# Short low-half products of two feed-forward units on the two row halves of the TensorE array

## The chip, the cores and the metric

The kernel runs on one core of a Trainium2 chip. The metric is the device time of the whole kernel in microseconds (us), taken as the median of several executions. One more execution is recorded by the hardware profiler; all views of the profile come from it.

## What is computed

The reference takes x (2048 tokens of 448 channels) and returns the sum of x, a spectral filter on its layer norm (a two-dimensional real FFT, a product with complex weights, and the inverse FFT), and a mixer with a feed-forward part:

```python
h = gelu(layernorm(x) @ w1)              # w1: 448 x 448
hs = shifted(h) @ w2                     # four channel groups, shifted by +1, -1, +2, -2 tokens
x1 = x + hs
h2 = gelu(layernorm(x1) @ w3) @ w4       # w3: 448 x 1792, w4: 1792 x 448
return x + spectral(layernorm(x)) + x1 + h2
```

## The kernel before

Single-precision products are made of half-precision ones: each operand is split into a high and a low half, and three of the four products are added in PSUM (high by high, weight high by data low, weight low by data high).

The work around the change is the feed-forward part. Its 2048 tokens form 8 groups `G` of 256, its 1792 hidden channels 7 pieces `fp` of 256; a *unit* is one pair (G, fp), so there are 56. For each unit, `front` makes the w3 products into one PSUM bank (128 hidden channels by 256 tokens, for two halves `ff`), and evacuates it: ACT applies the Gelu (L726) and takes the high half (L728), DVE takes the low half (L729). `back` then multiplies with w4 into the accumulators `acc` (L808). In groups 5, 6 and 7 some units (`SEVEN`) go through `sums` instead: the Gelu (L738) writes to SBUF, DVE forms sums (L740, L741), ACT and DVE split them (L744, L745), and `seven` (L778) makes seven smaller products in the place of eight. At the end of their group DVE adds these side sums to x (L786) and the accumulators too (L815).

The 448 rows of w3 are three blocks of 128 and one of 64. For the last 64 rows the tiles hold two copies: `w3p[:, 3]` (high halves) and `w3p[:, 7]` (low halves) hold rows 384 to 447 of w3 on partitions 0 to 63 and again on 64 to 127, and block 3 of `x2all` holds the data's high halves on partitions 0 to 63 and its low halves on 64 to 127. So two products are enough for this block, each over all 128 partitions, and a unit has 2 x (3 x 3 + 2) = 22 products, all recorded at the helper's line L400:

```python
for t in ts:
    for wi, xi in ((0, 0), (0, 4), (4, 0)) if t < 3 else ((0, 0), (4, 0)):
        T.matmul(ps_out, wp[:, wi + t, cols], xT[:, xi + t, tok],
                 start=t == 0 and wi + xi == 0, stop=t == 3 and wi == 4)
```

`mlp` runs the units of some groups. `ahead` says how many fronts are written before the back of a unit, `tags` which PSUM banks the fronts take in turn ("mm" has two banks, "mm" and "tr" together four). It is called five times: for group 0, for groups 1 and 2 (beside the forward transform, `step1`, L567), for groups 3 and 4 (beside the chunks, L622, L639 and L667, and their ACT and DVE work at L629, L630, L644, L655, L670), for group 5 (beside the inverse, L688 and L709), and for groups 6 and 7. Everything in `mlp` but the evacuations has the low priority `FILL`, so a scheduler that plays through a timeline ahead of the run puts these products wherever the work of higher priority leaves TensorE free; evacuations have the highest, `EVAC`. The order on each engine is then fixed. `behind(...)` asks that an instruction come after a given other one.

`ln2` prepares the data of the feed-forward part: it centres on POOL or ACT (L501, L499), splits, and writes `x2all` through a transposing DMA. `powers` (L260) and `w_scale_end` (L587, L591) contain a few tiny products that find scales.

Of the kernel before, what the change touches and what calls it, by code (L numbers as in the profile page):

```python
# [13 lines left out]
F16 = mybir.dt.float16  # L14
# [11 lines left out]
TURN = [3, 1, 0, 2]  # L26
DONE = {c: [c - 2] for c in range(2, 12)} | {12: [10, 13], 13: [11, 12, 14, 15]}
FIRST = 2
WARM = 26
ZPRE = 2.0 ** -7  # L30
UPRE = 2.0 ** -3
# [2 lines left out]
AH = 2  # L34
# [5 lines left out]
EVAC, FILL = 0, 100000  # L40
# [85 lines left out]
def body(tc, nc, x, wf, w1, w2, w3, w4, c_g, c_n, c_small, out):  # L126
    V, A, P, T, SY = nc.vector, nc.scalar, nc.gpsimd, nc.tensor, nc.sync
    PSUM = bass.MemoryType.PSUM

    @contextlib.contextmanager  # L130
    def prio(base):
        kept = tc.cur_priority
        tc.cur_priority = max(base, at.get(base, 0))
        yield
        at[base] = tc.cur_priority
        tc.cur_priority = kept
# [24 lines left out]
    pw = pool("pw")  # L161
# [6 lines left out]
    def xb(b):  # L168
        return xt[b // 2][:, b % 2]
# [4 lines left out]
    def at_token(b):  # L174
        return (b + FIRST) % NB

# [40 lines left out]
    def load_w3(ts):  # L217
        for t in ts:
            if t < 3:
                SY.dma_start(w3raw[:, t], w3[128 * t:128 * t + 128])  # L220
            else:
# [5 lines left out]
    load_w3([2])  # L227
    x2mem = pw.tile([128, 10 * F], F16, name="x2mem")
    x2all = [x2mem[:, 2 * F * j:2 * F * j + 2 * F].rearrange("p (t n) -> p t n", t=7) for j in (1, 0, 2, 3)]
    w4half = [x2mem.bitcast(F32)[:, 2 * F:2 * F + 4 * D].rearrange("p (f n) -> p f n", f=4),  # L230
              p1.tile([128, 10, D], F32, name="w4half")]
    w4v = w4.rearrange("(f p) n -> p f n", p=128)
# [139 lines left out]
    after = {}  # L372

    @contextlib.contextmanager
    def behind(*key):
        key = key if len(key) > 1 else key[0]
        with contextlib.ExitStack() as st:
            for i in after[key]:
                st.enter_context(tc.issue_after(i))
            yield  # L380
# [16 lines left out]
    def mlp_in(ps_out, wp, cols, xT, tok, ts=range(4)):  # L397
# [6 lines that stand above are left out]
    w3p = pa.tile([128, 8, F], F16, name="w3p")  # L404
# [77 lines left out]
    def ln2(bs, engines, late=None):  # L482

        n, b0 = len(bs), bs[0]
        mv = stats([xb(b) for b in bs], f"b{b0}")
        a = pc.tile([128, 4], F32, tag="vb", bufs=2, name=f"vb{b0}")[:, :n]
        r = pc.tile([128, 4], F32, tag="vs", bufs=2, name=f"vs{b0}")[:, :n]
        o, y = [], []
        nm = pc.tile([128, 4], F32, tag="nm", bufs=2, name=f"nm{b0}")[:, :n]
        P.tensor_scalar(out=nm, in0=mv[:, :n, 0], scalar1=-1.0, scalar2=None, op0=ALU.mult)  # L490
        for m in range(0, n, 2):
            w = stage(f"y{b0 + m}", 8 * 448, (b0 + m) // 2 % 2, F16)
            o.append(w[:, 0:4 * D].bitcast(F32).rearrange("p (i n) -> p i n", i=2))
            y.append(w[:, 4 * D:8 * D].rearrange("p (i n) -> p i n", i=2))
            for i in range(2):
                e = engines[m + i]
                c = nm[:, m + i:m + i + 1]
                if e is A:
                    A.activation(out=o[-1][:, i], in_=xb(b0 + m + i), func=AF.Identity, bias=c)  # L499
                else:  # L500
                    e.tensor_scalar(out=o[-1][:, i], in0=xb(b0 + m + i), scalar1=1.0, scalar2=c,  # L501
                                    op0=ALU.mult, op1=ALU.add)
        V.tensor_scalar(out=a, in0=mv[:, :n, 1], scalar1=eps12, scalar2=None, op0=ALU.add)
        rsqrt(r, a, n, f"b{b0}")
        for i in range(n):
            b, h, x_ = b0 + i, y[i // 2][:, i % 2], o[i // 2][:, i % 2]
            k = r[:, i:i + 1]
            with behind(*late) if late else contextlib.nullcontext():
                u = A.activation(out=h[:, 0:D], in_=x_, func=AF.Copy, scale=k)
            V.scalar_tensor_tensor(out=h[:, 448:512], in0=x_[:, 384:448], scalar=k, in1=h[:, 384:448],  # L510
                                   op0=ALU.mult, op1=ALU.subtract)
            v = V.scalar_tensor_tensor(out=h[:, 512:896], in0=x_[:, 0:384], scalar=k, in1=h[:, 0:384],
                                       op0=ALU.mult, op1=ALU.subtract)
            d = SY.dma_start_transpose(out=x2all[b // 4][:, :, 128 * (b % 4):128 * (b % 4) + 128], in_=h)
            after[f"b{b0}"] = u.ins, v.ins, d.ins

    def unscale(p, part):
        t = part.rearrange("p (b n) -> p b n", b=2)
# [194 lines left out]

    acc, hs = {}, {}

    def front(G, fp, tag):
        tok = slice(256 * (G % 2), 256 * (G % 2) + 256)
        pm = bank(tag, f"pw3_{G}{fp}")
        for ff in range(2):
            f = 2 * fp + ff  # L720
            mlp_in(pm[:, 256 * ff:256 * ff + 256], w3p, slice(128 * f, 128 * f + 128), x2all[G // 2], tok)
        with prio(EVAC):
            if fp in SEVEN.get(G, ()):
                hs[G, fp] = sums(G, fp, pm)
                return
            A.activation(out=pm, in_=pm, func=AF.Gelu_apprx_tanh, scale=r3)  # L726
            h = pw.tile([128, 2, 512], F16, tag="hf", bufs=3, name=f"hf{G}{fp}")
            i = A.activation(out=h[:, 0], in_=pm, func=AF.Copy, scale=h3)  # L728
            j = V.scalar_tensor_tensor(out=h[:, 1], in0=pm, scalar=h3, in1=h[:, 0], op0=ALU.mult, op1=ALU.subtract)  # L729
            after["f", G, fp] = i.ins, j.ins  # L730
        hs[G, fp] = h
# [56 lines left out]
    def back(G, fp):  # L788
        first, end = fp == ORD[G][0], fp == ORD[G][-1]
        if first:  # L790
            acc[G] = [bank("acc", f"acc{G}{i}") for i in range(2)]
            if G == 7:
                acc[G].append(bank("tr", "acc72"))
        h = None
        if fp in SEVEN.get(G, ()):
            seven(G, fp, end)
        else:
            h = hs.pop((G, fp))
        for i in range(2):
            b = 2 * G + i  # L800
            c = D // 2 if b == NB - 1 else D
            parts = [(slice(o, o + c), acc[G][i + o // c][:, 0:c]) for o in range(0, D, c)]
            for r, to in parts if h is not None else ():
                with behind("m", G, fp) if G == 7 and end and ("m", G, fp) in after else contextlib.nullcontext():
                    for f in (2 * fp, 2 * fp + 1):
                        for n, (hi, wi) in enumerate(PASS):
                            o = 256 * (f % 2) + 128 * i
                            m = T.matmul(to, h[:, hi, o:o + 128], w4p[0][:, wi, f, r],  # L808
                                         start=first and f % 2 == 0 and n == 0, stop=end and f % 2 == 1 and n == 2,
                                         skip_group_check=G in SEVEN)  # L810
                after["m", G, fp] = (m.ins,)
            if end:
                with prio(EVAC):
                    for r, to in parts:
                        V.scalar_tensor_tensor(out=xb(b)[:, r], in0=to, scalar=p34[:, min(G, 1):min(G, 1) + 1],  # L815
                                               in1=xb(b)[:, r], op0=ALU.mult, op1=ALU.add)
                        if G > 4:
                            SY.dma_start(ov[:, at_token(b), r], xb(b)[:, r])

    def mlp(Gs, hook=None, ahead=1, tags=("mm",)):  # L820
        with prio(FILL):
            todo = [(G, fp) for G in Gs for fp in ORD[G]]
            done = 0
            for n, (G, fp) in enumerate(todo):
                while done < min(n + 1 + (ahead if todo[n] != (7, 5) else 1), len(todo)):
                    front(*todo[done], tags[done % len(tags)])
                    if hook:
                        with prio(EVAC):
                            hook(*todo[done])
                    done += 1  # L830
                back(G, fp)


# [55 lines left out]
    n = 2  # L889
# [30 lines left out]
    with behind("g", 1), behind("na", 2):  # L920
        for k in range(4):
            r = slice(0, 128 if k < 3 else 64)
# [64 lines left out]
            with behind("f", G, fp):  # L987
                w4_split(2 * fp + 4)

    mlp([0], hook=w4_rest, ahead=AH, tags=("mm", "tr"))  # L990
    ln2(range(4, 8), [P, A, P, A])
    for b in range(8, 12):
        w2_tile(b)
# [23 lines left out]
            with behind("f", G, fp):  # L1017
                go()

    mlp([1, 2], hook=between, ahead=AH, tags=("mm", "tr"))  # L1020
    wl = stage("wl", 8 * DF, 1)
    for b in range(0, NB, 2):
        do_fold(b)
# [35 lines left out]
    for n in range(17):  # L1059
# [4 lines left out]
        if n:  # L1064
            b = bs[n - 1]
# [12 lines left out]
                    go()  # L1078

    mlp([5], hook=w4_late)  # L1080
    mlp(range(6, 8), hook=w4_late, ahead=2)
    for name in ("pv", "pz", "pa", "pw", "px", "pc", "ps"):
        close(name)

# [23 lines left out]
```

## Time and profile before

| | us |
|---|---|
| median of three runs | 408.19 |
| lowest and highest | 408.05, 408.2 |
| profiled execution, whole | 408.05 |
| profiled execution, first to last instruction (span) | 406.3 |

The clock that TensorE was granted is 0.998 of full speed on average. In the profile, PE is TensorE's products, PEld its weight loads, DVE VectorE, ACT ScalarE, POOL GpSimd and SP SyncE. A row of the timeline has start, length, engine, line, operation, destination and sources, shape and count; a merged row counts from the first start to the last end. A product's length is its latency: the next one starts before it ends, so rates are read from starts.

### The profile page before, as it was taken

The page shows a single profiled execution, that of the slowest core. Times are in us where ns is not written, and L with a number is a line of the kernel's source. Part 1 is how long each engine was busy: PE and PEld are TensorE (multiplying, and loading weights), DVE is VectorE, ACT ScalarE, POOL GpSimd, SP SyncE. Part 2 cuts the span into 40 slices and gives each one's busy share as a digit, 9 for nine tenths or more (in the row PEclk, how much of TensorE's full clock was granted, in tenths as well). Part 3 has the DMA queues.
Part 4 walks back from the last instruction along what each step waited for, and adds up shares of the span by engine and source line. Part 5 has one row for each costly group of instructions (what it writes and reads, how often), then busy time and mean ns, then how long its engine had stood idle before and what let it go on. Part 6 is the DMA issues. An engine that isn't in the chain of part 4 may idle for free.

```text
span 406.3 us, 8732 instructions
## 1 busy us (share of the span) xinstructions
PE 399.9 (98%) x3391; PEld 297.2 (73%) x3391; DVE 333.6 (82%) x702; ACT 255.1 (63%) x433; POOL 100.4 (25%) x158
## 2 busy tenths in 40 slices
PE   8999999999999999999999999999999999999996
PEld 3555555865667877777878878777677779998995
DVE  5898799898947887988698888965999999965645
ACT  4788889874568857655698878853354544353431
POOL 6859910111146946500021111110000000000000
PEclk9999999999999999999999999999999999999999
DMA  8978975567489661637256556510011023100101
GB/s 280 389 272 160 249 152 138 122 121 163 95 225 266 234 191 46 219 95 185 72 144 164 162 142 161 139 27 2 24 69 70 24 90 92 47 2 2 45 2 45
DMA packets 54596, 52.07 MB, mean 128 GB/s; under 512 B 35678, under 2 KB 48542, under 8 KB 54556
## 3 DMA queue, kind: packets, MB, share of 16 engines
q1 hardware_dynamic: 54556, 51.53, 46.0%
q8 instruction: 26, 0.43, 0.4%
q14 instruction: 14, 0.11, 0.1%
HBM read 38.28 MB, written 3.67 MB: 103 GB/s over the span
## 4 chain that ended last, share of the span: by engine, by line
PE 87%; POOL 5%; DMA 2%; DVE 2%; ACT 2%; issue 1%; SPq 0%; POOLq 0%; ACTq 0%
PE pw L400 33%; PE acc L808 23%; PE pw L478 6%; PE side L778 4%; PE acc L778 3%; PE pu L667 3%; PE ps L567 3%; PE pe L688 2%; PE pp L622 2%; PE px L639 2%; PE py L709 2%; PE pw L420 2%; DMA w1s<-w 1%; POOL xt L336 1%; DMA h<-x2mem 1%
## 5 line engine op out<-in xcount | busy, mean ns | idle before, releaser
L400 PE MATMUL pw<-x2mem,w3p 128*128 128x256 f16 x1232 | 151.3, 273 | 0.0
L400 PEld LDWEIGHTS <-w3p 128*128 128x128 f16 x1232 | 118.9, 98 | 19.3
L808 PE MATMUL acc<-w4p,hf 128*128 128x448 f16 (+1 forms) x516 | 104.4, 348 | 0.0
L808 PEld LDWEIGHTS <-hf 128*128 128x128 f16 x516 | 50.1, 98 | 37.6
L726 ACT ACTIVATE pw<-pw,pe 128x512 f32<-128x512 f32 x42 | 27.4, 654 | 26.8 <-PE pw L400 26.6
L729 DVE SCALAR_TENSOR_TENSOR hf<-pw,h,hf 128x512 f16<-128x512 f32 x42 | 31.3, 746 | 12.9 <-ACT hf L728 12.7
L478 PE MATMUL pw<-w2p,h 128*128 128x448 f16 x176 | 35.8, 353 | 0.9 <-DMA h<-x2mem 0.9
L420 PE MATMUL pw<-w1p,xT 128*128 128x448 f16 x176 | 34.9, 352 | 0.1
L648 POOL TENSOR_TENSOR z<-te 128x450 f32<-128x450 f32 x16 | 15.7, 983 | 70.8 <-DVE te L646 65.9
L728 ACT ACTIVATE hf<-pw,h 128x512 f16<-128x512 f32 x42 | 28.9, 687 | 5.0 <-PE acc L808 4.0
L478 PEld LDWEIGHTS <-h 128*128 128x128 f16 x176 | 17.0, 98 | 17.0 <-DMA h<-x2mem 2.0
L744 ACT ACTIVATE hz<-g,h 128x896 f16<-128x896 f32 x14 | 14.6, 1044 | 23.1 <-DVE g L741 23.1
L420 PEld LDWEIGHTS <-xT 128*128 128x128 f16 x176 | 17.1, 99 | 16.1 <-DVE xT L394 0.4
L778 PEld LDWEIGHTS <-hz 128*128 128x128 f16 x294 | 28.3, 98 | 0.6
L629 ACT ACTIVATE pf<-pp 64x450 f16<-64x450 f32 x32 | 17.4, 544 | 12.5 <-DVE pf L630 9.7
L630 DVE TENSOR_TENSOR pf<-pp,pf 64x450 f16<-64x450 f32 x32 | 19.9, 622 | 5.1 <-ACT pf L629 4.7
L745 DVE SCALAR_TENSOR_TENSOR hz<-g,h,hz 128x896 f16<-128x896 f32 x14 | 16.1, 1148 | 6.8 <-ACT hz L744 6.8
L550 POOL TENSOR_TENSOR f<-xr 128x452 f32<-128x452 f32 x16 | 19.7, 1251 | 0.6
L558 DVE TENSOR_TENSOR xh<-f,xh 128x452 f16<-128x452 f32 x16 | 14.3, 916 | 5.7 <-ACT xh L557 5.7
L644 ACT ACTIVATE te<-px 64x450 f32<-64x450 f32 x32 | 17.3, 541 | 1.2 <-PE px L639 0.6
L738 ACT ACTIVATE g<-pw,pe 128x512 f32<-128x512 f32 x14 | 9.6, 683 | 11.3 <-PE pw L400 11.3
L547 POOL TENSOR_TENSOR xr<-xf 128x452 f32<-128x452 f32 x8 | 9.2, 1156 | 22.3 <-issue 16.4
(188 smaller groups left out, 705.7 us busy)
## 6 DMA issues: line engine op xcount, KB each, us to landing
wc<-wf SPq DMA_DIRECT2D x32, 225.0 KB, 3.7
wl<-wf SPq DMA_DIRECT2D x8, 450.0 KB, 4.3
xt<-x SPq DMA_DIRECT2D x8, 448.0 KB, 7.1
xf<-x SPq DMA_DIRECT2D x8, 448.0 KB, 4.6
loads<-x SPq DMA_DIRECT2D x7, 448.0 KB, 4.0
out<-xt SPq DMA_DIRECT2D x13, 224.0 KB, 1.9
w3raw<-w SPq DMA_DIRECT2D x3, 896.0 KB, 10.8
gn<-c_g SPq DMA_DIRECT2D x16, 128.0 KB, 3.0
```

Source lines behind the costliest of these rows:

```text
L400: T.matmul(ps_out, wp[:, wi + t, cols], xT[:, xi + t, tok], start=t == 0 and wi + xi == 0, stop=t == 3 and wi == 4)
L420: m = T.matmul(pm[:, :D], xTs[g][:, xi + t, 128 * i:128 * i + 128], w1p[:, wi + t], start=t == 0 and p == 0, stop=t == 3 and p == 2)
L478: T.matmul(pm[:, :D], h[:, k], w2p[:, w], start=n == 0, stop=n == 10)
L550: P.tensor_tensor(out=f[:, :, k:k + 2].rearrange("p b s d -> p s b d"), in0=u[:, :, 0], in1=u[:, :, 1], op=op)
L629: A.activation(out=hi, in_=src, func=AF.Copy)
L630: V.tensor_tensor(out=lo, in0=src, in1=hi, op=ALU.subtract)
L644: A.activation(out=e[64 * h:64 * h + 64], in_=px_[64 - 64 * h:128 - 64 * h, :2 * DF], func=AF.Copy)
L726: A.activation(out=pm, in_=pm, func=AF.Gelu_apprx_tanh, scale=r3)
L728: i = A.activation(out=h[:, 0], in_=pm, func=AF.Copy, scale=h3)
L729: j = V.scalar_tensor_tensor(out=h[:, 1], in0=pm, scalar=h3, in1=h[:, 0], op0=ALU.mult, op1=ALU.subtract)
L778: m = T.matmul(to, h[:, hi, 128 * blk:128 * blk + 128], b[wi], start=new and n == 0, stop=n == 2 and (last if blk in (2, 5, 3, 0) else end ...
L808: m = T.matmul(to, h[:, hi, o:o + 128], w4p[0][:, wi, f, r], start=first and f % 2 == 0 and n == 0, stop=end and f % 2 == 1 and n == 2, sk ...
```

## The change

The low half of w3's last 64 rows is no longer multiplied with both halves of the data, but with the high half alone, over 64 partitions. The four such products of two neighbouring units (two halves `ff` each) are written one after another: the first unit's on partitions 0 to 63, the second's on 64 to 127, into different banks. For the second unit the data's high half is needed on partitions 64 to 127, so POOL copies it into a new tile `x2d`, once for each four blocks of tokens. A unit that has no partner (`alone`) keeps its 22 products. The two units of a pair are evacuated together, after the short products. `ahead` is 2 in all calls, where it was 1 for groups 3 to 5 and at one unit of group 7.

```diff
@@ body
+    x2d = pw.tile([128, 4, 512], F16, name="x2d")
@@ ln2
+        if b % 4 == 3:
+            P.tensor_copy(out=x2d[64:128, b // 4], in_=x2all[b // 4][0:64, 3])
@@ front
-    def front(G, fp, tag):
+    def front(G, fp, tag, alone):
         tok = slice(256 * (G % 2), 256 * (G % 2) + 256)
         pm = bank(tag, f"pw3_{G}{fp}")
         for ff in range(2):
             f = 2 * fp + ff
-            mlp_in(pm[:, 256 * ff:256 * ff + 256], w3p, slice(128 * f, 128 * f + 128), x2all[G // 2], tok)
+            for t in range(4):
+                for wi, xi in ((0, 0), (0, 4), (4, 0)) if t < 3 else ((0, 0), (4, 0)) if alone else ((0, 0),):
+                    m = T.matmul(pm[:, 256 * ff:256 * ff + 256], w3p[:, wi + t, 128 * f:128 * f + 128],
+                             x2all[G // 2][:, xi + t, tok], start=ff == 0 and t == 0 and wi + xi == 0,
+                                 stop=ff == 1 and t == 3 and wi == 4, skip_group_check=True)
+        after["w3"] = (m.ins,)
+        return pm
+
+    def last(units):
+        for ff in range(2):
+            for n, (G, fp, pm) in enumerate(units):
+                r = slice(64 * n, 64 * n + 64)
+                tok = slice(256 * (G % 2), 256 * (G % 2) + 256)
+                x_ = x2d[r, G // 2, tok] if n else x2all[G // 2][r, 3, tok]
+                f = 2 * fp + ff
+                with behind("w3"):
+                    m = T.matmul(pm[:, 256 * ff:256 * ff + 256], w3p[r, 7, 128 * f:128 * f + 128], x_, start=False,
+                                 stop=ff == 1, skip_group_check=True)
+
+    def evac(G, fp, pm):
         with prio(EVAC):
             ...
@@ mlp
-    def mlp(Gs, hook=None, ahead=1, tags=("mm",)):
+    def mlp(Gs, hook=None, ahead=2, tags=("mm",), single=1):
         with prio(FILL):
             todo = [(G, fp) for G in Gs for fp in ORD[G]]
-            done = 0
+            done, open_ = 0, []
             for n, (G, fp) in enumerate(todo):
-                while done < min(n + 1 + (ahead if todo[n] != (7, 5) else 1), len(todo)):
-                    front(*todo[done], tags[done % len(tags)])
-                    if hook:
-                        with prio(EVAC):
-                            hook(*todo[done])
+                while done < min(n + 1 + ahead, len(todo)):
+                    alone = not open_ and (done == len(todo) - 1 or done < single)
+                    open_.append((*todo[done], front(*todo[done], tags[done % len(tags)], alone)))
                     done += 1
+                    if alone or len(open_) == 2:
+                        if not alone:
+                            last(open_)
+                        for u in open_:
+                            evac(*u)
+                            if hook:
+                                with prio(EVAC):
+                                    hook(*u[:2])
+                        open_ = []
                 back(G, fp)
```

More of the change, by code (lines that the diff above doesn't have):

```diff
@@ L28 @@
 FIRST = 2
+HF = 3
 WARM = 26
@@ L726, in front @@
             A.activation(out=pm, in_=pm, func=AF.Gelu_apprx_tanh, scale=r3)
-            h = pw.tile([128, 2, 512], F16, tag="hf", bufs=3, name=f"hf{G}{fp}")
+            h = pw.tile([128, 2, 512], F16, tag="hf", bufs=HF, name=f"hf{G}{fp}")
             i = A.activation(out=h[:, 0], in_=pm, func=AF.Copy, scale=h3)
@@ L988, in w4_rest @@
                 w4_split(2 * fp + 4)
-    mlp([0], hook=w4_rest, ahead=AH, tags=("mm", "tr"))
+    mlp([0], hook=w4_rest, tags=("mm", "tr"))
     ln2(range(4, 8), [P, A, P, A])
@@ L1018, in between @@
                 go()
-    mlp([1, 2], hook=between, ahead=AH, tags=("mm", "tr"))
+    mlp([1, 2], hook=between, single=1, tags=("mm", "tr"))
     wl = stage("wl", 8 * DF, 1)
@@ L1080, in body @@
     mlp([5], hook=w4_late)
-    mlp(range(6, 8), hook=w4_late, ahead=2)
+    mlp(range(6, 8), hook=w4_late, single=1)
     for name in ("pv", "pz", "pa", "pw", "px", "pc", "ps"):
```

## The prediction

> **What bounds the kernel now.** I read the page first, then the table by stretches, the chain of waits, and single stretches of the timeline. The page says that one engine is full and which group fills it.
>
> ```profile
> span 406.3 us, 8732 instructions
> PE 399.9 (98%) x3391; PEld 297.2 (73%) x3391; DVE 333.6 (82%) x702; ACT 255.1 (63%) x433; POOL 100.4 (25%) x158
> PE 87%; POOL 5%; DMA 2%; DVE 2%; ACT 2%; issue 1%; SPq 0%; POOLq 0%; ACTq 0%
> ...
> L400 PE MATMUL pw<-x2mem,w3p 128*128 128x256 f16 x1232 | 151.3, 273 | 0.0
> L400 PEld LDWEIGHTS <-w3p 128*128 128x128 f16 x1232 | 118.9, 98 | 19.3
> ```
>
> TensorE (PE) is busy 98% of the span and carries 87% of the chain that ended last; L400, the w3 products that are changed, is its largest group and is never idle before an instruction (0.0). A busy PE could still run below its rate, so I look at starts. Three consecutive groups of the timeline, columns start and length:
>
> ```profile
> 132.98 2.56 PE L400 MATMUL pw<-x2mem,w3p 128*128 128x256 f16 x22
> 135.38 2.43 PE L808 MATMUL acc<-w4p,hf 128*128 128x448 f16 x12
> 137.65 1.50 PE L567 MATMUL ps<-csm,xh 128*128 128x128 f16 x24
> 138.99 2.56 PE L400 MATMUL pw<-x2mem,w3p 128*128 128x256 f16 x22
> ```
>
> From start to start, 22 w3 products of one unit take 2.40 us, 109.1 ns each; 12 w4 products 2.27 us, 189 ns each; 24 products of 128 columns, each with a weight load of its own, 1.34 us, 55.8 ns each. The groups follow each other without a gap. So a removed w3 product is worth 109 ns of the end time, not 273, which is its latency. The stretches say where something else is nearly full too (columns: sum PE, PEld, DVE, ACT, POOL, then clock, DMA share, GB/s):
>
> ```profile
> 195.00:283.00 88.00, 88.00 (x893) 70.63 (x891) 72.51 (x119) 67.23 (x120) 15.73 (x16) 1.00 0.44 117
> 283.00:345.00 62.00, 62.00 (x590) 48.49 (x588) 58.42 (x135) 28.66 (x52) 0.00 (x0) 1.00 0.18 61
> ```
>
> PE is busy for the whole of both, at clock 1.00. That cuts both ways: every slot saved counts, and every new wait counts too, since PE has no idle time to pay it from. DVE is at 94% from 283 to 345 us, and DVE and ACT at 82% and 76% from 195 to 283.
>
> **Products saved.** With one unit alone at the front of each of the five calls, and one at the end of the three calls with 14 units, 8 of the 56 units stay as they are and 48 form 24 pairs. A pair loses four full products (one for each half of two units) and gains four short ones. If the two row halves work at once, these take two slots: 4 x 109 - 2 x 109 = 218 ns less, 24 x 0.218 = **-5.2 us**. The four weight loads fit: at 55.8 ns each they need 223 ns.
>
> **Entering and leaving the half-array form.** No row shows 64-row products. The nearest are the two one-row products of L591; the same two-product step on all rows, L260, stands for comparison:
>
> ```profile
> 78.27 1.15 PE L400 MATMUL pw<-x2mem,w3p 128*128 128x256 f16 x9
> 79.26 0.28 PE L260 MATMUL pm<-pt,ones 128*128 128x1 f32 x2
> 79.40 0.92 PE L478 MATMUL pw<-w2p,h 128*128 128x448 f16 x4
> ...
> 189.61 1.11 PE L808 MATMUL acc<-w4p,hf 128*128 128x448 f16 x5
> 190.65 0.38 PE L591 MATMUL wpb<-wt,ones 1*128 1x1 f32 x2
> 190.96 0.74 PE L808 MATMUL acc<-w4p,hf 128*128 128x448 f16 x3
> ...
> 79.15 0.30 PEld L260 LDWEIGHTS pm<-pt,ones 128*128 128x128 f32 x2
> 79.29 0.77 PEld L478 LDWEIGHTS <-h 128*128 128x128 f16 x5
> 190.65 0.29 PEld L591 LDWEIGHTS wpb<-wt,ones 1*128 1x128 f32 x2 [0.37 <-issue]
> 190.95 0.49 PEld L808 LDWEIGHTS <-hf 128*128 128x128 f16 x4
> ```
>
> L260 starts where nine w3 slots end (78.27 + 9 x 0.109 = 79.25) and hands over 0.14 us later, at 79.40. L591 follows five w4 slots ending at 189.61 + 5 x 0.189 = 190.555, starts 0.095 us late, and hands over at 190.96: 0.405 us from end to start, 0.265 more. The load rows agree: the load after L260 starts while L260's loads run (79.29, inside 79.15 to 79.45), that after L591 only when they are over (190.95 after 190.94). So 0.265 us is the upper end of a trip into the short form and back; the lower is 0. I take 0.17 us, 0.095 in and a little less out; the rest I put down to the uncovered single-precision load, 0.30 us for two in L260's row, where L400 loads in 98 ns. 24 x 0.17 = **+4.1 us**, bounds 0 and 6.4. Below nothing is excluded: the trip adds no work that the full products had.
>
> The Trainium skill, TensorEngine Tiling (Array Packing), section Key Properties, says that changing the tiling mode drains the engine; the trace agrees, with those 0.095 us before L591. By the rule with that price for each change, the term would be 24 x 2 x 0.095 = 4.6 us in place of 4.1.
>
> **Groups torn apart.** The four short products are separate instructions of low priority; where the scheduler puts another product between them, a trip is paid again and an overlap lost. It does so to today's units:
>
> ```profile
> 226.13 0.27 PE L400 MATMUL pw<-x2mem,w3p 128*128 128x256 f16 x1
> 226.24 0.74 PE L639 MATMUL px<-pf,gn 128*128 128x225 f16 x6
> 226.82 0.38 PE L400 MATMUL pw<-x2mem,w3p 128*128 128x256 f16 x2
> 227.03 2.43 PE L808 MATMUL acc<-w4p,hf 128*128 128x448 f16 x12
> ```
>
> Here six chunk products stand before a unit's last two. I take two such breaks over the 12 or so pairs between 195 and 345 us, at 0.17 to 0.28 us: **+0.5 us**, bounds 0 and 2.
>
> **Later evacuation.** Today a unit is evacuated when its own products end, and before its bank is wanted again come one `back` and another `front`: 2.27 + 2.40 = 4.7 us. Paired, the first unit waits for the second and the short products, and then only one `back` (2.27 us) stands before the `front` that wants its bank, where units have just the two "mm" banks: groups 3, 4 and 5. Of the unit that ended at 227.03:
>
> ```profile
> 228.11 1.10 ACT L644 ACTIVATE te<-px 64x450 f32<-64x450 f32 x2
> 229.30 1.04 PE L400 MATMUL pw<-x2mem,w3p 128*128 128x256 f16 x8
> 229.68 0.64 ACT L726 ACTIVATE pw<-pw,pe 128x512 f32<-128x512 f32 x1
> 230.33 0.83 PE L667 MATMUL pu<-gn,zb 128*128 128x128 f16 x12
> 230.35 0.69 ACT L728 ACTIVATE hf<-pw,h 128x512 f16<-128x512 f32 x1
> 231.07 0.75 DVE L729 SCALAR_TENSOR_TENSOR hf<-pw,h,hf 128x512 f16<-128x512 f32 x1
> ```
>
> Its Gelu starts at 229.68, after other ACT work such as L644, and its bank is free when L729 ends, 231.82: 4.8 us after the products. The three steps themselves are 0.64 + 0.69 + 0.75 = 2.1 us, so even without a queue the chain just fits the 2.27 us. The next `front` starts at 229.30 today; it would wait 2.5 us here, unless chunk products such as L667 fill in. Those take about a third of PE between 195 and 283 us (28 us of 88: 286 w3 products at 0.109 and 152 w4 products at 0.189 leave that), so some 1.1 us stands beside each `back`. Between a need of 2.1 and 4.8 us and a cover of 3.4, I take 0.4 us a pair for the six pairs of groups 3 and 4, 2.4 us, and 0.6 us for the two such pairs of group 5, where DVE is at 94%. The counts just used:
>
> ```profile
> 195.00:283.00 88.00, 36.52 (x286) 27.21 (x287) 1.00 0.44 117
> 195.00:283.00 88.00, 31.53 (x152) 14.73 (x152) 1.00 0.44 117
> ```
>
> In groups 6 and 7 most units use the seven-product form. Their bank is free after the Gelu, but their halves come later:
>
> ```profile
> 380.62 2.57 PE L400 MATMUL pw<-x2mem,w3p 128*128 128x256 f16 x22
> 382.92 2.03 PEld L778 LDWEIGHTS <-hz 128*128 128x128 f16 x21
> 385.04 2.56 PE L400 MATMUL pw<-x2mem,w3p 128*128 128x256 f16 x22
> 386.13 1.15 DVE L745 SCALAR_TENSOR_TENSOR hz<-g,h,hz 128x896 f16<-128x896 f32 x1 [1.17 <-ACT hz L744]
> ```
>
> The unit's products end at 383.02 and L745 at 387.28, 4.26 us later. Today two backs and two fronts cover that; paired, one back (383.02 to 385.04, 2.02 us) and one front of 20 products (2.18 us), and the low half is wanted only by the third product: about even. I take 0.1 us a pair for six pairs, 0.6 us. In groups 0 to 2 units rotate over four banks: nothing. Together **+3.6 us**, bounds 0 and 9.
>
> **At nothing.** Four POOL copies of the high halves, each waiting for the transposes to land: POOL is busy 25%, and a unit alone and two fronts stand ahead of the first reader. Queued behind a copy on POOL are the next centring of `ln2` and the folds; if the folds came late, up to 1 us. ACT and DVE get as many instructions as before. The last unit is evacuated alone as today.
>
> **Sum.** -5.2 + 4.1 + 0.5 + 3.6 = +3.0 us on the profiled execution's 408.05, so 411.0; the median, 408.19, lies 0.14 above that execution, so **411.2 us**. By the bounds: from -5.2 to 1.2 + 2 + 9 + 1 = +13.2.
>
> **The rivals.** *The overlap is paid in full.* Trip free, breaks costing 0.2, waits 1.2 because chunk products fill them: -3.8, so 404.4. It decides once trip plus the rest is under 218 ns a pair; with my 4.1 us of breaks and waits, 0.17 us a pair, the trip must be under 0.05 us. For it: one-row single-precision products are a far stand-in for 64-row half-precision ones. Against: two independent rows point to a trip of over 0.1 us.
>
> *Loads of a half wait for that half's product.* The second product of each half then starts a load late, 98 ns for both halves together: 24 x 0.098 = +2.4, so 413.6. Full-array loads don't wait so (98 ns inside 109 in L400's two rows). This is the rule of the Trainium skill, TensorE: Matmul & The Clock Gate, section The mechanism: loads overlap running products only if the row group differs; no run here shows it for two groups.
>
> *The halves don't work at once.* Then the 5.2 us never come: +8.2, so 416.4. Nothing in this trace shows two products sharing the array.
>
> *It cancels.* A trip near 0.05 us with my waits leaves no change.
>
> **How the numbers follow.** About 0.2% (0.8 us) is what a measurement of this kernel tells from no change. Forecast 0.43, with a range of its own of 409.2 to 414; overlap in full, with its part ways, 0.27; loads that wait 0.12; no overlap 0.12; cancelling 0.06. Slower is 0.43 + 0.12 + 0.12 = 0.67. The range leaves the outermost tenth of each side: 403.9 to 417.0.
>
> **What would show it.** The short products get their own line: in each group of four, the second should start within about 60 ns of the first, and the step from the last full product's slot to the next full product should last 0.39 us. PE should show idle time before `front` in the stretch from 195 to 345 us, released by DVE's last step of an evacuation (today's L729). It would be wrong if the groups last under 0.3 us and PE stays gapless (faster), or if the second short product starts a full 109 ns after the first.

## The result, and the profile after

The changed kernel takes 413.60 us (four runs, 412.83 to 414.29) against 408.12 us before; the ratio is 1.0135, with a 95% interval of 1.0115 to 1.0155. The forecast was 411.2 us, in a range of 403.9 to 417.0. The profiled execution of the changed kernel took 413.91 us, with a span of 412.1 us, 5.8 us more than the span before; line numbers have moved (the full w3 products are L729 now, the short ones L743, the w4 products L833, the last evacuation step L754, the POOL copy L519).

The page of the changed kernel: span, busy time, the chain that ended last by engine, and the group of the full w3 products with its loads.

```profile
span 412.1 us, 8721 instructions
PE 402.2 (98%) x3391; PEld 288.7 (70%) x3391; DVE 334.3 (81%) x702; ACT 249.7 (61%) x433; POOL 103.9 (25%) x162
PE 51%; DVE 5%; ACT 5%; issue 4%; POOL 1%; DVEq 0%; POOLq 0%; ACTq 0%
...
L729 PE MATMUL pw<-x2mem,w3p 128*128 128x256 f16 x1136 | 138.6, 273 | 0.4 <-DVE hf L754 0.4
L729 PEld LDWEIGHTS <-w3p 128*128 128x128 f16 x1136 | 109.9, 98 | 19.6 <-DVE hf L754 0.8
```

PE is still full by its busy share, but its part of the chain has shrunk. The 51% can't be set beside the 87% as they stand, for here the chain can be followed back only to 137.7 us, over 66% of the span (before, over 99%). From 138.6 us on, PE had 99.8% of the chain before and has 77% of it now; at many places it goes through DVE, ACT and issue. The idle time before the w3 products was 0.0 and now is 0.4. The list of waits says the same (who waited for whom: total, times, longest); before, PE waited for none of these:

```profile
PE acc L833 <- DVE hf L754: 1.4, 1, 1.4
...
PE px L643 <- DVE te L649: 0.5, 1, 0.5
PE ps L571 <- DVE y L576: 0.4, 1, 0.4
PE pu L671 <- DVE y L675: 0.4, 1, 0.4
PE pw L729 <- DVE hf L754: 0.4, 1, 0.4
```

These count only time in which PE is empty. Measured from start to start, and adding up what each step lasts beyond its product's own slot, from 60 us on and without the short groups, it is 5.1 us against 0.7 us before.

What the change is about is one group of four short products. The timeline of the changed kernel:

```profile
147.21 1.25 PE L729 MATMUL pw<-x2mem,w3p 128*128 128x256 f16 x10
148.40 0.28 PE L743 MATMUL pw<-x2mem,w3p 64*128 64x256 f16 x1
148.40 0.28 PE L743 MATMUL pw<-x2d,w3p 64*128 64x256 f16 x1
148.51 0.27 PE L743 MATMUL pw<-x2mem,w3p 64*128 64x256 f16 x1
148.52 0.27 PE L743 MATMUL pw<-x2d,w3p 64*128 64x256 f16 x1
148.72 1.50 PE L833 MATMUL acc<-w4p,hf 128*128 128x448 f16 x7
```

The ten full products end their slots at 147.21 + 10 x 0.109 = 148.30; the first short one starts at 148.40. The two halves start together (3 to 4 ns apart, unrounded), the second two 0.12 us later, and the next full product only 0.20 us after the last short one, where a slot would be 0.109. In unrounded starts of the 21 whole groups: 96 ns in, then 3, 116 and 3 ns, 202 ns to the next full product, which itself takes 10 ns longer. That is 431 ns for what took 4 x 109 = 436 ns. The two halves overlap, and the trip into the half-array form and back costs 431 - 2 x 109 = 213 ns, the two slots saved but for 5 ns. A group is *whole* when its four short products follow each other, and *torn* when other products stand between them; three of the 24 are torn.

The span's 5.8 us are, by the trace:

| part | us |
|---|---|
| 21 whole groups, 431 in place of 436 ns | -0.1 |
| three torn groups | +0.9 |
| waits of PE after 60 us, 5.1 for 0.7 | +4.4 |
| from the last product's start to the end, 4.0 for 3.6 | +0.4 |
| gaps in the first 60 us, 8.7 for 8.5 | +0.2 |

### The profile page after: what moved, and what is told of

The parts are those of the page before. It is cut to its first block, busy times and chain, and to the rows that moved or that the text cites. A ratio compares the mean times of both kernels' runs of the same rounds, so it can differ in the third digit from the quotient of the medians.

```text
span 412.1 us, 8721 instructions
## 1 busy us (share of the span) xinstructions
PE 402.2 (98%) x3391; PEld 288.7 (70%) x3391; DVE 334.3 (81%) x702; ACT 249.7 (61%) x433; POOL 103.9 (25%) x162
## 4 chain that ended last, share of the span: by engine, by line
PE 51%; DVE 5%; ACT 5%; issue 4%; POOL 1%; DVEq 0%; POOLq 0%; ACTq 0%
PE pw L729 19%; PE acc L833 13%; PE side L803 4%; PE acc L803 3%; PE pe L692 2%; PE py L713 2%; PE ps L571 2%; ACT te L648 2%; PE pu L671 1%; PE px L643 1%; PE pp L626 1%; PE pw L743 1%; ACT pf L633 1%; POOL f L554 1%; DVE xt L811 1%
## 5 line engine op out<-in xcount | busy, mean ns | idle before, releaser
L729 PE MATMUL pw<-x2mem,w3p 128*128 128x256 f16 x1136 | 138.6, 273 | 0.4 <-DVE hf L754 0.4
L729 PEld LDWEIGHTS <-w3p 128*128 128x128 f16 x1136 | 109.9, 98 | 19.6 <-DVE hf L754 0.8
L833 PE MATMUL acc<-w4p,hf 128*128 128x448 f16 (+1 forms) x516 | 107.4, 348 | 1.5 <-DVE hf L754 1.4
L833 PEld LDWEIGHTS <-hf 128*128 128x128 f16 x516 | 48.1, 98 | 40.8 <-issue 2.7
L754 DVE SCALAR_TENSOR_TENSOR hf<-pw,h,hf 128x512 f16<-128x512 f32 x42 | 30.7, 743 | 11.3 <-ACT hf L753 11.2
L751 ACT ACTIVATE pw<-pw,pe 128x512 f32<-128x512 f32 x42 | 26.2, 651 | 16.3 <-PE pw L743 9.0
L753 ACT ACTIVATE hf<-pw,h 128x512 f16<-128x512 f32 x42 | 28.0, 685 | 4.7 <-PE acc L833 4.5
L554 POOL TENSOR_TENSOR f<-xr 128x452 f32<-128x452 f32 x16 | 18.8, 1197 | 0.6
L561 ACT ACTIVATE xh<-f 128x452 f16<-128x452 f32 x16 | 8.4, 570 | 16.9 <-POOL f L554 16.9
L562 DVE TENSOR_TENSOR xh<-f,xh 128x452 f16<-128x452 f32 x16 | 13.5, 880 | 6.0 <-ACT xh L561 6.0
L705 ACT ACTIVATE vh<-e 128x448 f16<-128x448 f32 x16 | 8.9, 573 | 13.7 <-DVE e L703 11.5
```

Of the source, the lines that this page charges most:

```text
L554: P.tensor_tensor(out=f[:, :, k:k + 2].rearrange("p b s d -> p s b d"), in0=u[:, :, 0], in1=u[:, :, 1], op=op)
L729: m = T.matmul(pm[:, 256 * ff:256 * ff + 256], w3p[:, wi + t, 128 * f:128 * f + 128], x2all[G // 2][:, xi + t, tok], start=ff == 0 and t = ...
L833: m = T.matmul(to, h[:, hi, o:o + 128], w4p[0][:, wi, f, r], start=first and f % 2 == 0 and n == 0, stop=end and f % 2 == 1 and n == 2, sk ...
```

## The experiments

Theory A: the trip eats the saving, and the loss is waits and torn groups. Rival B: the overlap does save about 5 us, and waits of some 10 us hide it. Under A it is open where the waits come from: C, the POOL copies; D, the paired evacuation.

### Full rows in the place of the short ones

```diff
-                r = slice(64 * n, 64 * n + 64)
-                x_ = x2d[r, G // 2, tok] if n else x2all[G // 2][r, 3, tok]
+                r = slice(0, 128)
+                x_ = x2all[G // 2][r, 3, tok]
```

> The four short products of a pair are made over all 128 partitions instead (low weights with high and low data, as before the change), at the same place and with the same paired evacuation and the same copies. Theory A, the trip into the half-array form eats the saving (a whole group measures 431 ns against 436 for four full products) and the loss is waits plus three torn groups: about 412.8, 0.9 less than the changed kernel, and waits of PE as there. Rival B, the overlap saves its 5.2 us and larger waits hide that: about 418.6.

Measured: 416.84 us, ratio 1.0218 [1.0203, 1.0233]. Neither number came. The edit also freed the second unit from `x2d`, and the scheduler wrote another order; the timeline of this kernel shows what that did:

```profile
115.17 0.67 ACT L501 ACTIVATE y<-xt,nm 128x448 f32<-128x448 f32 x1 [5.74 <-DMA x2mem<-y]
115.75 1.22 ACT L751 ACTIVATE pw<-pw,pe 128x512 f32<-128x512 f32 x2
117.63 0.93 PE L833 MATMUL acc<-w4p,hf 128*128 128x448 f16 x4 [2.14 <-ACT hf L753]
```

ACT stands 5.7 us at a centring (L501) that waits for a transposing DMA; the Gelus of a pair (L751) are queued behind it, and PE stands 2.1 us for the high halves (L753). The changed kernel has no such wait there. So this run doesn't separate A from B; it shows that a pair's evacuation behind one late instruction costs microseconds. A comparison in the same order was needed, and follows below.

### The copies by DMA

```diff
-            P.tensor_copy(out=x2d[64:128, b // 4], in_=x2all[b // 4][0:64, 3])
+            SY.dma_start(x2d[64:128, b // 4], x2all[b // 4][0:64, 3])
```

> The four copies of the high halves are made by the DMA queue of SyncE instead of POOL. Theory C, POOL's queue behind the copies (10.8 and 5.8 us of waiting for transposes) delays the third centring and the folds, and so causes the 2.5 us of PE waits between 140 and 160 us: about 411.1, the folds back near their times before the change, these waits gone. Rival D, the waits come from the paired evacuation alone: 413.6, unchanged.

Measured: 411.42 us, ratio 1.0083 [1.0068, 1.0098], as theory C had it. The waits between 140 and 160 us are gone. POOL in the changed kernel, first from its list of waits, then from its timeline, the last copy and the second fold:

```profile
POOL x2d L519 <- DMA x2mem<-y: 19.5, 4, 10.8
...
128.12 1.51 POOL L519 COPY x2d<-x2mem 64x512 f16<-64x512 f16 x1 [5.81 <-DMA x2mem<-y]
129.72 1.06 POOL L551 TENSOR_TENSOR xr<-xf 128x452 f32<-128x452 f32 x1
```

The same fold with the copies on the DMA queue:

```profile
124.86 1.58 POOL L551 TENSOR_TENSOR xr<-xf 128x452 f32<-128x452 f32 x1 [2.61 <-issue]
```

The four copies last 0.6 to 1.5 us each, but POOL stands 19.5 us in front of them. Not all of that is lost, since without the copies POOL stands longer at other steps; what counts is that the second fold comes 4.9 us later than here. How this reaches PE is seen in the changed kernel's timeline (all of DVE's steps, and those of ACT and PE that matter):

```profile
150.79 2.39 DVE L562 TENSOR_TENSOR xh<-f,xh 128x452 f16<-128x452 f32 x2 [0.83 <-ACT xh L561]
152.75 1.27 ACT L753 ACTIVATE hf<-pw,h 128x512 f16<-128x512 f32 x2
153.10 0.68 DVE L576 TENSOR_TENSOR y<-ps,y 128x512 f16<-128x512 f32 x1
153.70 1.27 DVE L524 SCALAR_TENSOR_TENSOR xt<-xt,s,loads 128x896 f32<-128x896 f32 x1
154.89 1.08 DVE L274 TENSOR_REDUCE wm<-wl 128x1 f32<-128x900 f32 x1
155.89 1.40 DVE L754 SCALAR_TENSOR_TENSOR hf<-pw,h,hf 128x512 f16<-128x512 f32 x2
156.69 1.12 PE L833 MATMUL acc<-w4p,hf 128*128 128x448 f16 x5 [1.39 <-DVE hf L754]
```

DVE works the late folds off (L562, which had itself waited, by way of ACT's L561), then three steps queued behind (L576, L524, L274), and only at 155.89 the low halves of a pair whose high halves ACT had finished by 154.0. PE stands 1.4 us.

### The copies alone, in the kernel before

```diff
+        if b % 4 == 3:
+            P.tensor_copy(out=x2d[64:128, b // 4], in_=x2all[b // 4][0:64, 3])
```

> The kernel before with the four POOL copies added, their result unused. Theory C: the folds come late here too, 409 to 410.5 (less than 2.5 us are lost, since single units leave PE more to do). Rival D: 408.2, no change.

Measured: 411.21 us, ratio 1.0081 [1.0064, 1.0098]: 3.2 us for four instructions whose result nobody reads, more than theory C's 2.3 at most. The profiled execution is the fastest of the four, 410.28 us, 2.2 us over the one before; its trace shows 1.9 us of new PE waits between 140 and 147 us. The last 0.9 us of the median stand in no trace. So the copies are no matter of the pairs: on POOL's queue they cost microseconds in both kernels. In the changed kernel their price is 2.2 us (413.60 to 411.42).

### The same half for all four

```diff
-                r = slice(64 * n, 64 * n + 64)
-                x_ = x2d[r, G // 2, tok] if n else x2all[G // 2][r, 3, tok]
+                r = slice(0, 64)
+                x_ = x2all[G // 2][r, 3, tok]
```

> All four short products of a pair on partitions 0 to 63 (the values are the same, since both halves of the weight tile hold the same rows). If the two halves truly work at once in the changed kernel, a group grows from 96 + 3 + 116 + 3 + 202 + 10 to about 96 + 3 x 116 + 202 + 10 = 656 ns: 24 x 0.225 = 5.4 us more, 419.0. Rival: a limit per product rather than per half (loads, issue) sets the 116 ns, and one half does as well: 413.6.

Measured: 420.67 us, ratio 1.0306 [1.0291, 1.0322]. A whole group lasts 646 ns in this trace, 215 more than with two halves: that is the overlap. The rest of the difference isn't, for this kernel has the free order of the first one (416.84) with its waits.

### The paired evacuation alone

Full rows as in the first run, and no copies:

```diff
-        if b % 4 == 3:
-            P.tensor_copy(out=x2d[64:128, b // 4], in_=x2all[b // 4][0:64, 3])
```

> The paired evacuation alone: the low products over all 128 partitions as in the first run with full rows, and no copies at all. Theory E, without copies the paired order costs about 2 us of PE waits between 195 and 345 us (1.9 us were left with the copies on the DMA queue) and 0.4 us at the end: about 410.6. Rival, the order on ACT and DVE that made PE wait 2.3 us at 115 us and 3.5 us between 140 and 160 us with full rows belongs to the paired evacuation and not to the copies: about 415 to 417.

Measured: 413.07 us, ratio 1.0121 [1.0104, 1.0137], between the two. Without copies and without short products, pairing, with fronts written two ahead, costs 4.9 us in this order: a wait of 1.4 us remains at 115 us, and 2.2 us between 220 and 310 us. The waits of 140 to 160 us are gone, so they belong to the copies.

### No pairs

```diff
-    def mlp(Gs, hook=None, ahead=2, tags=("mm",), single=1):
+    def mlp(Gs, hook=None, ahead=2, tags=("mm",), single=99):
```

> Every unit alone with its 22 products and evacuated by itself, no copies; what stays of the change is that two fronts are written ahead in all calls (one, before, in groups 3 to 5 and at one unit of group 7). If writing further ahead costs nothing: 408.1, within 0.5. If it is what makes PE wait between 240 and 310 us: about 410.

Measured: 408.78 us, ratio 1.0016 [1.0006, 1.0025]; no new PE wait after 60 us. Writing further ahead is not what makes PE wait. Of the 0.6 us, 0.4 are at the end, where 4.0 us pass after the last product's start in place of 3.6; the last experiment shows why. The other 0.2 us lie outside the span: an execution is 1.88 to 1.99 us longer than its span here, and 1.68 to 1.76 before.

### Four buffers

```diff
-HF = 3
+HF = 4
```

(with the copies on the DMA queue)

> As the run with the copies on the DMA queue, with four buffers for the halves hf in place of three. If the buffers held back the paired evacuations: the waits between 240 and 260 us (1.4 us) go, 410.0. If the banks and the ACT and DVE queues hold them back: 411.4, unchanged.

Measured: 411.38 us, ratio 1.0078 [1.0063, 1.0093], the same as with three (411.42). The buffers of the halves hold nothing back. Which of the others does can be read in part from the changed kernel's timeline, at its three longest waits after 200 us:

```profile
248.46 0.84 PE L671 MATMUL pu<-gn,zb 128*128 128x128 f16 x12 [0.37 <-DVE y L675]
...
258.43 0.74 PE L643 MATMUL px<-pf,gn 128*128 128x225 f16 x6 [0.47 <-DVE te L649]
...
307.98 2.36 PE L729 MATMUL pw<-x2mem,w3p 128*128 128x256 f16 x20 [0.37 <-DVE hf L754]
```

The first two, which make most of the waits between 240 and 260 us, stand before chunk products: these wait until DVE has read their own banks (`pu` by L675, `px` by L649), and not for a bank of the fronts. Only the third is a front that waits for an evacuation. So in groups 3 and 4 it is the chunk steps on DVE that come late; that the two evacuations of a pair, one behind the other on ACT and DVE, make them late is argued and wasn't tried.

### The same order: full rows, and one half

To keep the order, the copy is widened so that the second unit still depends on `x2d`. Instructions of PE, DVE, ACT and POOL stand in the same order as with the copies by DMA.

```diff
-            SY.dma_start(x2d[64:128, b // 4], x2all[b // 4][0:64, 3])
+            SY.dma_start(x2d[:, b // 4], x2all[b // 4][:, 3])
-                r = slice(64 * n, 64 * n + 64)
+                r = slice(0, 128)
```

> The run with the copies on the DMA queue (411.4 us), with the same order of instructions on TensorE, VectorE, ScalarE and GpSimd, but each of the four low products over all 128 partitions (the copy takes 128 partitions instead of 64, so that the second unit still depends on it). Theory A, the trip eats the overlap: 24 groups of 436 ns in place of 21 of 431 and three torn ones that cost 0.9 us more: 410.6. Rival B, the overlap saves about 5 us: 416.5.

Measured: 410.04 us, ratio 1.0047 [1.0032, 1.0062], against 1.0083 [1.0068, 1.0098] with short products. In the same order, the kernel with four full products is *faster* than the one with four overlapping short ones, by some 1.4 us. The timeline of this kernel has 0.109 us from each to the next, and no step in or out:

```profile
145.62 1.26 PE L729 MATMUL pw<-x2mem,w3p 128*128 128x256 f16 x10
146.71 0.27 PE L743 MATMUL pw<-x2mem,w3p 128*128 128x256 f16 x1
...
147.15 2.43 PE L833 MATMUL acc<-w4p,hf 128*128 128x448 f16 x12
```

From 145.62 + 1.09 to 147.15 are 0.44 us for the four. Torn groups, which cost nothing here, explain 0.9 us of the difference; by whole groups the short form is ahead by 5 ns each. The two profiled executions differ by another 0.7 us in the gaps of the first 60 us, where neither has a group; these gaps vary between 8.3 and 9.2 us over the traces of all runs, so this part says nothing of the short form.

```diff
-            SY.dma_start(x2d[64:128, b // 4], x2all[b // 4][0:64, 3])
+            SY.dma_start(x2d[0:64, b // 4], x2all[b // 4][0:64, 3])
-                r = slice(64 * n, 64 * n + 64)
+                r = slice(0, 64)
```

> As the run with the copies on the DMA queue, same order of instructions on every engine, with all four short products on partitions 0 to 63. If the two halves work at once: 21 whole groups of 646 in place of 431 ns, 4.5 us, and about 0.3 us in the torn ones: 416.2. If the same half does as well: 411.4.

Measured: 415.21 us, ratio 1.0176 [1.0159, 1.0193]: 3.8 us over the overlapping form where 4.8 was expected. Its timeline:

```profile
157.73 1.47 PE L729 MATMUL pw<-x2mem,w3p 128*128 128x256 f16 x12
159.13 0.33 PEld L743 LDWEIGHTS <-w3p 64*128 64x128 f16 x4 [0.21 <-issue]
159.14 0.28 PE L743 MATMUL pw<-x2mem,w3p 64*128 64x256 f16 x1
159.26 0.27 PE L743 MATMUL pw<-x2d,w3p 64*128 64x256 f16 x1
159.37 0.27 PE L743 MATMUL pw<-x2mem,w3p 64*128 64x256 f16 x1
159.47 0.27 PE L743 MATMUL pw<-x2d,w3p 64*128 64x256 f16 x1
159.68 2.44 PE L833 MATMUL acc<-w4p,hf 128*128 128x448 f16 x12
```

The four come one after another now, 0.12 and then 0.11 us apart, 646 ns a group; the groups add the 4.8 us, and the waits between 240 and 260 us shrink from 1.4 to 0.5 us, since PE comes later to what it waited for.

### Eight short products in a group

```diff
-        for ff in range(2):
+        for rep, ff in ((0, 0), (0, 1), (1, 0), (1, 1)):
```

> Every short product is made twice, so that a group has eight instead of four (the low part of the last 64 rows is counted twice); copies on the DMA queue. If the trip is paid once a group: a whole group lasts 431 + 2 x 119 = 669 ns, and the marginal cost of two overlapping short products is 119 ns; 417.1 if the waits stay as they are. If each product pays part of the trip: a group lasts about 860 ns and the time is about 421.7.

Measured: 419.5 us, in one run alone, so without an interval; the argument rests on its trace. A whole group:

```profile
148.43 1.26 PE L729 MATMUL pw<-x2mem,w3p 128*128 128x256 f16 x10
149.62 0.28 PE L743 MATMUL pw<-x2mem,w3p 64*128 64x256 f16 x1
...
149.96 0.27 PE L743 MATMUL pw<-x2d,w3p 64*128 64x256 f16 x1
150.16 2.06 PE L833 MATMUL acc<-w4p,hf 128*128 128x448 f16 x10
```

From 149.52, the end of the full slots, to 150.16 are 0.64 us, 650 ns with the 10 ns after it: 219 ns more than a group of four, two slots for four products. So the trip is paid once a group, and the two weight loads of each further pair fit into its 109 ns. The time is above the expected 417.1 us because more groups are torn (32 pieces for 24 pairs, where it was 27) and PE waits 2.1 us more between 260 and 280 us.

### Pairs where no wait was

Pairs in groups 6 and 7 only, `ahead` and single units before that as they were, one copy by DMA:

```diff
+    mlp([0], hook=w4_rest, tags=("mm", "tr"), single=99)
+    mlp([1, 2], hook=between, single=99, tags=("mm", "tr"))
+    mlp(range(3, 5), ahead=1, single=99)
+    mlp([5], hook=w4_late, ahead=1, single=99)
```

> Pairs in groups 6 and 7 only, where the changed kernel shows no PE wait; one copy, by SyncE's DMA queue; groups 0 to 5 as before the change. Six pairs. Theory A (a group is worth its trip): 408.1, or 408.5 with one torn group of +0.3. Rival B (the overlap saves, 0.218 each): 406.9.

Measured: 409.45 us, ratio 1.0030 [1.0017, 1.0043]. Not the 406.9 of rival B; 0.9 us above A.

```diff
-                while done < min(n + 1 + ahead, len(todo)):
+                while done < min(n + 1 + (ahead if todo[n] != (7, 5) else 1), len(todo)):
-                with behind("w3"):
+                with behind("w3"), prio(EVAC):
```

> The run with pairs in groups 6 and 7 only, with the short products at the high priority, so that no group is torn, and with the last front written after the back of unit (7, 5) again, as before the change. Theory A: neither torn groups (0.3) nor the later end (0.4 to 0.5) remain, so 408.2, no change from before; it can't be faster by more than 0.1. Rival B: 406.9.

Measured: 409.08 us, ratio 1.0025 [1.0016, 1.0035]. All six groups are whole, and the last product starts at 402.72 us (402.75 before): for PE the pairs are worth nothing, as A says. But the time is still 0.25% up, 1.1 us, and the end shows where half of it comes from. DVE's side sums and last additions before, and in this kernel:

```profile
395.79 3.74 DVE L786 SCALAR_TENSOR_TENSOR xt<-side,p,xt 128x896 f32<-128x896 f32 x5 [1.57 <-PE side L778]
401.90 1.60 DVE L815 SCALAR_TENSOR_TENSOR xt<-acc,p,xt 128x448 f32<-128x448 f32 x3 [1.25 <-PE acc L808]
```

```profile
398.51 3.73 DVE L811 SCALAR_TENSOR_TENSOR xt<-side,p,xt 128x896 f32<-128x896 f32 x5
402.34 1.40 DVE L840 SCALAR_TENSOR_TENSOR xt<-acc,p,xt 128x448 f32<-128x448 f32 x3
```

Unit (7, 5) is paired with (7, 3), and the last front still comes ahead of its back; so the side sums start at 398.51 instead of 395.79, run until 402.24, and the last additions, which had waited for PE, wait for them. That makes 4.1 us from the last product's start to the end in place of 3.6. The kernel without pairs has the same end. Another 0.4 us lie outside the span: an execution is 2.11 to 2.19 us longer than its span here and 1.67 to 1.75 before (2.11 to 2.21 in the run before this one). Why that is stays open. No version tried here beats the kernel before.

## Why the prediction was right, and where its terms were off

The direction and the main reason held: PE had no idle time, the overlap's saving was spent on entering and leaving the half-array form, and waits made the rest. The size is in part luck. Of the span's 5.8 us the prediction had 3.0: it was 1.4 us too low on the groups (trip and torn ones) and 1.7 us too high on the evacuations it named, which nearly cancel; the copies, put at nothing, are most of what it is short of. The median came to 413.60 us for the 411.2 forecast. Its terms:

- **Products saved, -5.2 us.** Right: the halves start 3 to 4 ns apart, and one half alone makes a group 215 ns longer (218 said). That the four loads fit did not follow from its own figures, 223 ns in two slots of 218; the groups of eight show that they do.
- **The trip, 0.17 us, +4.1.** Mis-sized: 213 ns, so +5.1 were all 24 groups whole. The entry of 96 ns is what the one-row products showed (0.095); the way out is 93 + 10 ns, and some 13 ns more lie inside the group. Of the 0.265 us upper end I put too much down to single precision. By the Trainium skill, TensorEngine Tiling (Array Packing), section Key Properties, a change of mode drains the engine; the trace agrees in that both changes cost time, 96 ns in and about 103 out. Whether a drain is all that these pauses are made of, the rows don't tell: the first short load, too, starts only at the end of the pause (159.13 on one half, after 0.21 us without a load).
- **Torn groups, +0.5 for two.** Three, at +0.9. One in the changed kernel, at 324.72 to 326.09:

```profile
324.72 0.52 PE L692 MATMUL pe<-csm,U 113*128 113x113 f16 x7
325.17 0.28 PE L743 MATMUL pw<-x2mem,w3p 64*128 64x256 f16 x1
325.18 0.28 PE L743 MATMUL pw<-x2d,w3p 64*128 64x256 f16 x1
325.39 0.55 PE L713 MATMUL py<-vh,csm 128*128 128x448 f16 x2
325.87 0.28 PE L743 MATMUL pw<-x2mem,w3p 64*128 64x256 f16 x1
325.88 0.28 PE L743 MATMUL pw<-x2d,w3p 64*128 64x256 f16 x1
326.09 0.93 PE L833 MATMUL acc<-w4p,hf 128*128 128x448 f16 x4
```

- **Later evacuation, +3.6.** The waits come to 4.4 us in all, near it by luck; the places are others. In groups 3 and 4 1.35 us came for 2.4, in group 5 0.5 for 0.6, in groups 6 and 7 none for 0.6; in groups 1 and 2, which I had at nothing for their four banks, 2.5 us, and those go with the POOL copies. The mechanism held in group 5 alone: a `front` that waits for its bank until L754 has ended (307.98). In groups 3 and 4 PE waits before chunk products, for DVE steps of the chunks.
- **At nothing: the POOL copies.** This is the step that failed. I named what is queued behind them and gave up to 1 us; they cost 2.2 us here and 3.2 alone. I took POOL's 25% busy time for slack, but the price is set by the waiting ahead of the copies and by who stands in the queue behind: the second fold came 4.9 us late.
- **The end, at nothing.** It cost 0.4 us: the last front before the back of (7, 5) also sets when DVE's side sums start.

Of the rivals, the overlap paid in full would have needed a trip under 0.05 us; it is four times that. The halves do work at once. And loads of one half don't wait for that half's product: four in a row on one half start 120 and then 109 ns apart, and their four loads all lie between 159.13 and 159.46 us, while the products run. So that rival's 413.6 us is the measured time by chance. Here the measurement speaks against the rule as the Trainium skill, TensorE: Matmul & The Clock Gate, section The mechanism, lists it, that loads overlap running products only if the row group differs; a sentence above it in that section excepts loads into a background weight buffer.

## What to carry to other kernels

Price a partial-array form by the stay, that is by one whole visit from entering to leaving, not by the product: here a stay costs 213 ns, two products of 256 columns, and each two overlapping products save one, so four only break even, and the eight that took 650 ns stand against 872 ns for eight full ones. Before adding a small instruction to an engine that is idle most of the time, look at what it must wait for and at what stands behind it in that queue; four copies of 0.6 us cost 3.2 us in the kernel before. And when the order of instructions is computed, compare in the same order: with full rows and no copies on POOL, the kernel whose second unit depends on the copied tile takes 410.04 us, and the one that is free of it 413.07.

## What the runs showed of the hardware

- Entering the 64-row form after full products lasts 96 ns beyond the slot, after groups of any kind; the next full product starts 202 ns after the last short one (212 after a stay of a single slot), for a slot of 109.
- Two short products on different row halves, into different banks, start 3 to 4 ns apart; from the start of one such pair to the next are 119 ns at first and 109 later (groups of eight).
- The price of a stay does not depend on how many products are in it: 431 ns with four and 650 with eight leave 213 and 214 ns beyond two and four slots, and a torn pair of two, 322 ns, leaves 213 beyond one.
- Four products on the same row half, each with its own load, start 120, 109 and 109 ns apart, the plain slot but for the first step; the second load (159.15 to 159.24 us) runs while the first product does.
